# An attention block with a gated MLP: folding the softmax sums on GpSimd, and a new order of the first projections

## The chip, the cores and the metric

The kernel runs on one core of a Trainium2 chip. The metric is the device time of one launch in microseconds (us), the median of several runs. Engines in the profile: PE is TensorE (PEld its weight loads), DVE is VectorE, ACT is ScalarE, POOL is GpSimd, SPq is the queue that issues transfers.

## The reference, cut to what matters

```python
h = layernorm(x) * (1 + ca) + sa                  # x: 2048 rows of 1024, bf16; modulation from c @ w_mod
q = (h @ wq) as 32 heads of 32;  k = h @ wk;  v = h @ wv     # one key and value head for all
p = softmax(q k^T / sqrt(32));   o = p v
x = x + ga * (o @ wo)
h = layernorm(x) * (1 + cb) + sb
x = x + gb * ((silu(h @ w1) * (h @ w3)) @ w2)      # 3584 wide
```

Two pieces set the work: 2048 x 2048 exponentials for each of 32 heads (ScalarE), and the matmuls (TensorE).

## The kernel before

The queries are taken in eight blocks of 256 rows, the heads in eight groups `f` of four. One step is one score tile pair: 8 score matmuls of two key tiles against four heads, and two exps of 128x1024 that write a tile of 128x2048 in bf16. Eight steps make a head group. The MLP of one block runs as filler between the scores of the next.

A program at build time simulates the engines with assumed durations and fixes, for each engine, the order of its instructions. On the chip every engine works through its list in that order, with waits on semaphores. So an assumed duration decides only about order; the chip decides about time.

The softmax denominator is the sum of the exps over keys. VectorE first adds exp tiles in two trees of four, then folds the second tree into the first; TensorE multiplies the result with a matrix of ones and zeros (`SEL`) to sum over partitions:

```python
# in step(): the tree
G.add("dve", ... TR[tr] = U[first] + U[u] ...)            # L942
G.add("dve", ... TR[tr] = TR[tr] + U[u] ...)              # L948
# ...
def finish(f, h=None):
    trs = trees[f]
    if h is None and f in FOLD:                            # FOLD = groups 0 to 6
        ta, tb = trs
        G.add("dve", lambda e, ta=ta, tb=tb: e.tensor_tensor(
            TR[:, ta, 0:4 * W], TR[:, ta, 0:4 * W], TR[:, tb, 0:4 * W], ALU.add), ...)   # L957, 128x2048
        trs = trs[:1]
    # ... the value matmuls of this group, then the sums of the group before:
    def dmm(e, ...):
        for x in range(len(td) * npk):                     # npk = 2 key tiles side by side
            for gg in range(4):
                e.matmul(PB[g.bank][32 * gg:32 * gg + 32, qn:2 * qn], SEL[:, ga, gj, :],
                         a[:, (gg * npk + x % npk) * qn:...], ..., tile_position=(0, 32 * gg))
```

The kernel uses eight banks of PSUM, the on-chip memory that the matmuls here write to; SBUF is the other one, which holds inputs and results. While attention runs, six banks hold scores and two (`PB0`, `PB1`) serve everything else: the filler matmuls, the values and the sums. VectorE empties these two.

The softmax here doesn't subtract the row's maximum and nothing guards it: scores larger than these inputs give would overflow.

## Time and profile before

| | kernel before |
|---|---|
| time, median of 3 runs before the prediction | 1160.13 us (1158.57 to 1160.46) |
| span of the profiled run | 1158.1 us |
| first exp, last exp | 29.2 us, 1047.7 us |
| a full block of 256 queries | 126.1 us |
| TensorE, ScalarE, VectorE busy in it | 125.7, 125.6, 117.0 us |
| after the last exp | 110.4 us, TensorE alone |

The table's rows are read from the busy time by stage and from the timeline of the exps; the prediction shows the lines. The VectorE groups are rows of the instruction table: line, engine, operation, output and inputs, shapes, count, then total busy us, mean ns of one, and idle time before them.

```profile
L948 DVE TENSOR_TENSOR UREG<-UREG 128x2048 bf16<-128x2048 bf16 x240 | 292.8, 1220 | 12.8 <-ACT UREG L925 10.8
L942 DVE TENSOR_TENSOR UREG<-UREG 128x2048 bf16<-128x2048 bf16 x120 | 146.4, 1220 | 11.5 <-PE PB L1002 6.4 <-ACT UREG L925 5.0
L1158 DVE SCALAR_TENSOR_TENSOR HREG<-GSB,HREG 128x512 bf16<-128x512 bf16 x56 | 38.4, 685 | 0.3
L1153 DVE TENSOR_TENSOR HREG<-GSB,PB 128x512 bf16<-128x512 bf16 x52 | 35.5, 683 | 3.3 <-PE PB L1141 3.2
L1042 DVE TENSOR_TENSOR QT<-XN 128x256 bf16<-128x256 f32 x64 | 26.7, 421 | 0.3
L1124 DVE TENSOR_SCALAR QT<-QT,MODC 128x256 bf16<-128x256 bf16 x48 | 13.2, 342 | 0.0
```

Read the input side: `UREG`, `XN`, `QT`, `GSB`, `HREG` lie in SBUF, `PB` in PSUM. The tree adds, the gating product L1158 and the division L1042 have two inputs in SBUF; L1153 has one in SBUF and one in PSUM; the scaling L1124 has one tensor input, in SBUF.

### The profile page before, as it was taken

To read this page: it belongs to the slowest core of one execution; us is meant where nothing else is said; L and a number is where in the kernel's file an instruction comes from. 1 tells how busy PE (TensorE), PEld (TensorE's weight loads), DVE (VectorE), ACT (ScalarE), POOL (GpSimd) and SP (SyncE) were. 2 spreads that over 40 slices of the span, in tenths; PEclk is the share of its full clock that TensorE was granted. 3 is DMA by queue.
4 is the path that set the end of the run, shared out by engine and by line. 5 is a ranking of instruction groups with operands and counts; after the bars stand their busy time and mean duration, and the time that the engine had idled before them with its cause. 6 is when DMAs were issued, how large, how long until landed. Compare 5 with 4: busy or idle time off the path is not lost.

```text
span 1158.1 us, 35702 instructions
## 1 busy us (share of the span) xinstructions
PE 1122.6 (97%) x15918; PEld 767.1 (66%) x15918; DVE 984.7 (85%) x1498; ACT 1027.6 (89%) x1170; POOL 43.5 (4%) x86
## 2 busy tenths in 40 slices
PE   7799998999979999999999999999999999999998
PEld 6564444776646766777577766776677766777887
DVE  5837889999888999899999998999989999997452
ACT  5789999999999999999999999999999999992110
POOL 3200001000000001000100001000100010000000
PEclk8899999999989999999999999999999999999999
DMA  9337005956546565856496567766586649756996
GB/s 331 113 129 220 19 2 127 275 169 178 166 122 190 169 193 149 248 170 192 119 279 196 159 177 194 226 169 174 152 252 181 185 122 258 204 152 192 284 291 160
DMA packets 385417, 211.10 MB, mean 182 GB/s; under 512 B 21744, under 2 KB 376048, under 8 KB 385264
## 3 DMA queue, kind: packets, MB, share of 16 engines
q1 hardware_dynamic: 383184, 208.69, 64.5%
q8 instruction: 125, 2.05, 0.8%
q10 hardware_dynamic: 2080, 0.13, 0.1%
q14 instruction: 28, 0.23, 0.1%
HBM read 201.46 MB, written 4.19 MB: 178 GB/s over the span
## 4 chain that ended last, share of the span: by engine, by line
PE 92%; ACT 3%; DVE 3%; DMA 1%; SPq 1%; issue 0%; POOL 0%; DVEq 0%
PE PB L1141 33%; PE PB L1175 16%; PE SP L915 14%; PE PB L975 11%; PE PB L1107 5%; PE PB L658 4%; PE SP L1141 3%; ACT UREG L925 3%; PE SP L1175 2%; PE PB L1002 2%; DMA UREG<-in_w_mod_dram 1%; PE PB L637 1%; PE PB L838 0%; PE SP L1107 0%; DVE WO L850 0%
## 5 line engine op out<-in xcount | busy, mean ns | idle before, releaser
L925 ACT ACTIVATE UREG<-SP 128x1024 bf16<-128x1024 f32 x1024 | 968.6, 1075 | 18.8 <-PE SP L915 16.4
L948 DVE TENSOR_TENSOR UREG<-UREG 128x2048 bf16<-128x2048 bf16 x240 | 292.8, 1220 | 12.8 <-ACT UREG L925 10.8
L915 PE MATMUL SP<-QT,KT 32*128 32x256 bf16 x4096 | 204.8, 274 | 16.0 <-ACT UREG L925 15.0
L1141 PE MATMUL PB<-QT,WREG 128*128 128x256 bf16 x1648 | 207.4, 274 | 1.8 <-DVE DSB L1026 1.6
L1141 PEld LDWEIGHTS PB<-QT,WREG 128*128 128x128 bf16 x1648 | 150.1, 98 | 46.8 <-issue 31.2
L942 DVE TENSOR_TENSOR UREG<-UREG 128x2048 bf16<-128x2048 bf16 x120 | 146.4, 1220 | 11.5 <-PE PB L1002 6.4
L915 PEld LDWEIGHTS SP<-QT,KT 32*128 32x128 bf16 x4096 | 61.2, 93 | 138.6 <-ACT UREG L925 79.6
L1141 PE MATMUL PB<-QT,HREG 128*128 128x256 bf16 x1056 | 133.7, 274 | 0.8 <-DVE DSB L1026 0.8
L975 PE MATMUL PB<-UREG,V 128*32 128x256 bf16 x4032 | 132.2, 277 | 1.7 <-DVE QT L610 0.9
L975 PEld LDWEIGHTS PB<-UREG,V 128*32 128x32 bf16 x4032 | 99.3, 98 | 27.5 <-issue 17.9
L1141 PEld LDWEIGHTS PB<-QT,HREG 128*128 128x128 bf16 x1056 | 96.1, 98 | 29.7 <-issue 19.6
L1175 PE MATMUL PB<-WREG,HREG 128*128 128x256 bf16 x812 | 101.2, 273 | 0.0
L1175 PEld LDWEIGHTS PB<-WREG,HREG 128*128 128x128 bf16 x812 | 75.3, 98 | 20.4 <-issue 11.4
L1175 PE MATMUL PB<-HREG 128*128 128x256 bf16 x532 | 67.8, 274 | 0.0
L1141 PE MATMUL PB<-QT,X 128*128 128x256 bf16 x528 | 67.8, 274 | 0.0
L658 PE MATMUL PB<-HREG,WREG 128*128 128x512 bf16 (+1 forms) x312 | 64.1, 343 | 0.3 <-DVE DSB L1026 0.3
L957 DVE TENSOR_TENSOR UREG<-UREG 128x2048 bf16<-128x2048 bf16 x52 | 63.4, 1220 | 0.5
L1150 ACT ACTIVATE GSB<-GSB 128x512 bf16<-128x512 bf16 x56 | 38.8, 693 | 27.5 <-DVE GSB L1148 27.5
L1014 DVE COPY XN<-PB 128x256 f32<-128x256 f32 x63 | 26.6, 422 | 39.6 <-PE PB L1002 39.3
L1175 PEld LDWEIGHTS PB<-HREG 128*128 128x128 bf16 x532 | 49.2, 98 | 14.3 <-issue 8.0
L1107 PE MATMUL PB<-WO,QT 128*128 128x512 bf16 x232 | 57.6, 381 | 0.2 <-DVE QT L661 0.2
L1141 PEld LDWEIGHTS PB<-QT,X 128*128 128x128 bf16 x528 | 48.2, 98 | 14.3 <-issue 9.3
(139 smaller groups left out, 1031.9 us busy)
## 6 DMA issues: line engine op xcount, KB each, us to landing
WREG<-in_B_w_dram SPq DMA_DIRECT2D x112, 512.0 KB, 5.1
HREG<-in_B_w_dram SPq DMA_DIRECT2D x74, 512.0 KB, 5.2
WREG<-in_B_w_dram SPq DMA_DIRECT2D x33, 896.0 KB, 5.1
X<-in_B_w_dram SPq DMA_DIRECT2D x38, 512.0 KB, 5.1
HREG<-in_B_w_dram SPq DMA_DIRECT2D x21, 896.0 KB, 5.2
X<-in_B_w_dram SPq DMA_DIRECT2D x10, 896.0 KB, 5.1
X<-in_A_x_dram SPq DMA_DIRECT2D x32, 256.0 KB, 5.0
WREG<-in_w_mod_dram SPq DMA_DIRECT2D x16, 512.0 KB, 4.7
```

Of the source, the lines that this page charges most:

```text
L658: g = mm_group(NC, lambda e, b, c: e.matmul(b[:, 0:n], WQ[:, c, f * P:(f + 1) * P], HT[:, c, sl], start=c == 0, stop=c == NC - 1), lambda ...
L915: r = e.matmul(SP[:, b, o:o + qn], KT[32 * gg:32 * gg + 32, kts[j] * P:(kts[j] + 1) * P], QT[32 * gg:32 * gg + 32, f, q0:q0 + qn], start=T ...
L925: G.add("act", lambda e, u=u, h0=h0, n=n, b0=b0, nb=nb: e.activation(U[:, u, h0 * W:(h0 + n) * W].rearrange("p (b w) -> p b w", b=nb), SP[ ...
L942: G.add("dve", lambda e, tr=tr, u=u, fu=first_u: e.tensor_tensor(TR[:, tr, 0:4 * W], U[:, fu, 0:4 * W], U[:, u, 0:4 * W], ALU.add), reads= ...
L948: G.add("dve", lambda e, tr=tr, u=u: e.tensor_tensor(TR[:, tr, 0:4 * W], TR[:, tr, 0:4 * W], U[:, u, 0:4 * W], ALU.add), reads=[("TR", tr) ...
L957: G.add("dve", lambda e, ta=ta, tb=tb: e.tensor_tensor(TR[:, ta, 0:4 * W], TR[:, ta, 0:4 * W], TR[:, tb, 0:4 * W], ALU.add), reads=[("TR", ...
L975: r = e.matmul(PB[g.bank][32 * gg:32 * gg + 32, 0:qn], V[:, kt, :], U[:, pu, (gg * npk + j) * qn:(gg * npk + j + 1) * qn], start=w0 + n == ...
L1014: G.add("dve", lambda e, g=g, f=f: e.tensor_copy(ASB[:, f % 4, 0:qn], PB[g.bank][:, 0:qn]), writes=[("ASB", f % 4), ("XN", 2 + f % 4 // 2) ...
L1107: g = mm_group(NC, lambda e, b, f, t=t, h=h: e.matmul(b, QT[:, f, t * P:(t + 1) * P], WO[:, f, h * 512:(h + 1) * 512], start=f == 0, stop= ...
L1141: return e.matmul(b[:, j * qn:(j + 1) * qn], w13[:, w, c, j * P:(j + 1) * P], QT[:, c, q0:q0 + qn], start=c == 0, stop=c == NC - 1)
L1150: G.add("act", lambda e, b=b: e.activation(TB[b], GS[b], ACT.Tanh, scale=0.5), reads=[("GS", b)], writes=[("TB", b)], clear=alias("TB") if ...
L1175: G.add("pe", lambda e, g=g, j=j, fc=fc, hf=hf, first=first, w2s=w2s: e.matmul(PB[g.bank][:, j * 256:(j + 1) * 256], HHT[:, hf * NH + fc, ...
```

## The change

It has two parts. First, 48 of 52 folds move from VectorE to GpSimd, which is idle, as two adds of half the width; a third GpSimd add folds the two key tiles side by side, so that TensorE streams 4 sum matmuls per head group instead of 8. Second, the first projections: priorities of the first queries, bias adds and late layer norms, the PSUM banks of the first key projections, and warm-up matmuls of 512 columns instead of 128.

```diff
+    POOLT = 0.0022                               # assumed us per element on GpSimd
+    DFOLD = [(QB, f) for f in range(4)]          # four folds stay on VectorE
...
             if h is None and f in FOLD:
                 ta, tb = trs
-                G.add("dve", lambda e, ta=ta, tb=tb: e.tensor_tensor(
-                    TR[:, ta, 0:4 * W], TR[:, ta, 0:4 * W], TR[:, tb, 0:4 * W], ALU.add), ...)
+                pool = (q0, f) not in DFOLD
+                parts = 2 if pool else 1
+                for k in range(parts):
+                    a, b = k * 4 * W // parts, (k + 1) * 4 * W // parts
+                    G.add("pool" if pool else "dve", lambda e, ta=ta, tb=tb, a=a, b=b: e.tensor_tensor(
+                        TR[:, ta, a:b], TR[:, ta, a:b], TR[:, tb, a:b], ALU.add), ...)
+                if pool and npk == 2:
+                    tv = TR[:, ta, 0:4 * W].rearrange("p (g j q) -> p g j q", g=4, j=2)
+                    G.add("pool", lambda e, tv=tv: e.tensor_tensor(tv[:, :, 0], tv[:, :, 0], tv[:, :, 1], ALU.add), ...)
+                    nx = 1
...
-                    for x in range(len(td) * npk):
+                    for x in range(len(td) * nx):
...
-    kproj(512, 512, (1,))
+    kproj(512, 512, (6, 7))
...
-    qproj(0, 256, 1, (0, 1))
+    qproj(0, 256, 1, (0, 1), prio=1)
     vproj(0, (0, 1))
+    qproj(0, 256, 2, (0, 1), prio=1)
     vproj(1, (0, 1))
...
-    G.warm = (WARM, P / 2400.0 + 0.0026, warm, ident)
+    G.warm = (WARM, MM, warm, ident, 26.0)
```

(Cuts marked with "..."; left out are priorities and the plumbing of `nx`.)

## The prediction

> **What bounds the kernel now.** I read the page's busy table first, then the busy time by stage. The eight query blocks of 256 rows have a period of 126.1 us, so I cut the windows at the first exp (29.2), at the block starts and at the last exp (1047.7). Columns: stretch, length, PE, PEld, DVE, ACT, POOL busy, granted clock, DMA share, GB/s.
>
> ```profile
> PE 1122.6 (97%) x15918; PEld 767.1 (66%) x15918; DVE 984.7 (85%) x1498; ACT 1027.6 (89%) x1170; POOL 43.5 (4%) x86
> ```
>
> ```profile
> 29.20:62.00 32.80, 26.37 (x556) 17.24 (x556) 26.36 (x72) 22.61 (x25) 6.65 (x16) 0.90 0.42 119
> 62.00:184.00 122.00, 117.34 (x1763) 59.80 (x1756) 89.67 (x138) 119.36 (x127) 0.00 (x0) 1.00 0.26 82
> ...
> 310.50:436.60 126.10, 117.14 (x1669) 77.52 (x1665) 114.20 (x166) 124.39 (x142) 3.48 (x4) 0.96 0.59 164
> ...
> 562.70:688.80 126.10, 125.70 (x1812) 85.84 (x1804) 117.04 (x171) 125.59 (x143) 3.43 (x4) 1.00 0.69 189
> ...
> 1047.70:1158.10 110.40, 106.00 (x1012) 91.57 (x1009) 53.03 (x95) 10.94 (x19) 1.69 (x4) 1.00 0.89 233
> ```
>
> The reader sees two engines full at once: in a steady block TensorE is busy 125.7 and ScalarE 125.6 of 126.1 us. VectorE has 9 us free, GpSimd nearly all. After the last exp TensorE alone runs 110 us (rest of the seventh MLP, the last block). So the end is: last exp, plus the TensorE work left then. Over all stages TensorE idles 35.5 us, and ScalarE 18.3 us between first and last exp. The timeline says where:
>
> ```profile
> 35.60 7.44 ACT L925 ACTIVATE UREG<-SP 128x1024 bf16<-128x1024 f32 x8 [2.56 <-PE SP L915]
> ...
> 61.86 19.00 ACT L925 ACTIVATE UREG<-SP 128x1024 bf16<-128x1024 f32 x20 [5.57 <-PE SP L915]
> ...
> 325.16 0.40 PE L915 MATMUL SP<-QT,KT 32*128 32x256 bf16 x8 [1.43 <-ACT UREG L925]
> 326.99 0.40 PE L915 MATMUL SP<-QT,KT 32*128 32x256 bf16 x8 [1.44 <-ACT UREG L925]
> ```
>
> In the head ScalarE starves (10.2 us between 29 and 62, half of it one gap before 61.86), because projections and transposes stand ahead of the scores in TensorE's order. At 325 the reverse: seven score steps stand without filler between them, and TensorE waits 1.2 to 1.4 us at each.
>
> **What the Trainium skill says.** "SBUF — State Buffer", section "Who interferes with whom": VectorE and GpSimd share one port pair; a VectorE instruction with two SBUF inputs, or in a 2-port mode, and a GpSimd instruction that reads SBUF exclude each other for the whole instruction. The trace agrees in one direction:
>
> ```profile
> 569.85 1.23 DVE L942 TENSOR_TENSOR UREG<-UREG 128x2048 bf16<-128x2048 bf16 x1
> 569.99 1.16 POOL L551 TENSOR_SCALAR RS<-MV 128x1 f32<-128x1 f32 x1 [119.41 <-DVE MV L532]
> ...
> 1064.42 0.22 POOL L551 TENSOR_SCALAR RS<-MV 128x1 f32<-128x1 f32 x1 [109.39 <-DVE MV L532]
> ```
>
> The same one-column instruction takes 0.22 us alone and 1.16 beside an add, ending when the add ends. The other direction, a long GpSimd instruction that stops an add, does not occur here: no GpSimd work is long enough.
>
> "GPSIMD Engine Reference", section 3.1 "Elementwise — side-by-side cycle accounting": about 2.6 cycles per element for a two-input add at 1.2 GHz, so by estimate 1024 x 2.6 / 1.2 = 2.2 us for 1024 elements. No such add is in the trace.
>
> "TensorE: Matmul & The Clock Gate", Part 1: an idle window of some 3.4 us halves the clock. The trace agrees roughly: scores of 0.40 us become 0.61 after the waits at 325, and the clock of that stage is 0.96, in the head 0.90.
>
> **The change, part by part.**
>
> 1. *Sum matmuls.* The built order has 608 against ones instead of 800: for 48 of 52 folded head groups, 4 instead of 8. Four run side by side in array columns, and of the same shape
>
> ```profile
> L1002 PE MATMUL PB<-UREG,SEL 128*32 128x256 bf16 x776 | 31.8, 275 | 0.0
> ```
>
> ```profile
> 148.94 1.86 PE PB L975 x64
> ```
>
> the chain of waits gives 1.86 / 64 = 29 ns each (the 275 of the first line, a group of the instruction table, is latency). Removed: 192 x 29 ns = **5.6 us** of TensorE, 0.8 us per block. All of it lies in the full stage.
>
> 2. *Folds.* VectorE loses 48 adds of 1.22 us (58.6 us; 8 per block). GpSimd gains 96 half-adds and 48 key-tile adds, each of 1024 elements: 144 x 2.2 = 317 us by the estimate, 46 per block. GpSimd's own share, 4% to about 31%, is no bound. A fold of 3 x 2.2 = 6.6 us instead of 1.2 has to be done by the next head group's sums, one period of 126.1 / 8 = 15.8 us later, so latency alone is hidden.
>
> 3. *Order of the first projections.* Queries 1 to 3 rise to scores' rank, their bias adds go first on VectorE, late layer norms too. In the built order the first MLP tanh comes after 184 exps instead of 168, so scores run 8 steps further ahead; the run of seven bare score steps at 325 is one of three. I expect the 5.6 us gap to close and about 2.5 of the other 4.6 us in the head: **-8 us** at ScalarE. The first score has the same work in front of it, so 29.2 stays. Warm-up matmuls of 512 columns, a little closer packed, only fill idle time; I give them nothing of their own.
>
> 4. *Tail.* After the last score matmul stand 45 gate/up matmuls where there were 2 (and 20 sum matmuls for 24). The chain has 80 of them in 8.73 us, 0.109 us each: 43 x 0.109 = **+4.7 us** of filler moved behind the last exp.
>
> *Sums.* ScalarE's side: -8 in the head, -2 from smaller waits in five full blocks (at most 126.1 - 125.6 = 0.5 each), +4.7 in the tail: -5.3 us. TensorE's side: -5.6 sums, -5.8 for four bare steps fewer at 1.44, some -2 of idle in the head: -13. Both must be met; the later one sets the end. ScalarE's -5.3 would be 1155; but how much of its 10 us in the head closes is my least certain term (all 10.2 would give -7.5, 1152.6). I choose 7 us gain: **1153 us**.
>
> **Rivals.**
>
> *A, the shared port makes VectorE the bound.* In the steady block, VectorE work that needs the pair is: tree adds 58.6, gating products 9.6, divisions 3.4, residual adds 1.7, two-port scalings 3.3: 77 us. With 46 us of GpSimd that is 123 of 126 us under one lock. VectorE's room is 9 idle + 8 removed = 17 us, or 0.8 us for each of the 21 GpSimd pieces of a block. If each piece holds VectorE for what remains after one short PSUM instruction (0.7 us; 2.2 - 0.7 = 1.5 us), 31 us are lost and 14 not covered: over six or seven blocks +80 to +100, about 1240. For it: the exclusion seen above, two thirds of the block's VectorE time needing the pair. Against it: about half the VectorE instructions (80 of 171 in the block) have at most one SBUF input and can run beside GpSimd; seen so far is only GpSimd waiting; the folds are cut in halves and four are left on VectorE in one block, as if somebody had measured; a tuned kernel rarely takes a step that costs 7%. A milder form: each hold delays a PSUM read, and TensorE, with two PSUM banks for filler and 0.4 us of slack per block, cannot catch up; 0.1 us per piece is 2 us per block, 14 in all: 1165.
>
> *B, nothing gained: ScalarE is the bound anyway.* In full blocks it has 0.5 us free, so the 5.6 us of matmuls could turn into idle TensorE time and the head's gain be handed back in the tail: 1158 to 1161. For it: 125.6 of 126.1 busy. Against it: TensorE alone fills the last 110 us and its total work counts there.
>
> *C, the head closes wholly.* ScalarE's idle time of 18.3 us shrinks to 3 or 4 and the clock does not drop: last exp 14 us earlier, +4.7: 1149 to 1151, a few us less if cold time is won back.
>
> **Range and chances.** Main line and C span 1147 to 1157, B to 1161, the milder A to 1168. Eight in ten: 1143 to 1168. Full A gets 9%; below 1137 needs more than 20 us, more than ScalarE's idle time allows even with the tail unchanged: 3%. Within 2%: 88%.
>
> **What would show it.** Right: sum matmuls' busy time down by a quarter; exps without a gap over 3 us from 29 on; last exp at 1037 to 1042; block period 125.6 to 126.1; GpSimd's adds near 2.2 us, VectorE's adds still near 1.22; some 115 us after the last exp. A: adds of VectorE over 2 us, VectorE near 100% busy or idle at GpSimd's release, a longer block period, TensorE waiting for VectorE or GpSimd before projections and sums. B: TensorE idle in steady blocks up by 0.8 us, the end unmoved. C: the stage 29 to 62 with ScalarE over 90% busy. The prediction is wrong above all if GpSimd's instructions hold VectorE for their whole length, or if they take much longer than 2.2 us because they wait for VectorE, so that the sums come late.

## The result, and the profile after

The changed kernel takes **1266.82 us** (1264.17 to 1268.32, 4 runs) against 1159.35 us in the same rounds: 9.2% slower, ratio 1.0924, 95% interval 1.0907 to 1.0941. (A ratio here is the mean time of one kernel's runs over that of the other's in the same rounds, so not quite the ratio of the medians quoted.)

The page's busy line, then four stages, cut at the first and the 129th exp, and later near every further 128th (within two exps), in the columns of the prediction's table of stages:

```profile
PE 1144.6 (91%) x15643; PEld 756.4 (60%) x15643; DVE 1084.3 (86%) x1450; ACT 1033.8 (82%) x1170; POOL 394.9 (31%) x230
```

```profile
27.50:156.80 129.30, 117.72 (x1987) 64.30 (x1987) 94.83 (x168) 119.86 (x130) 27.92 (x25) 0.99 0.35 112
156.80:292.70 135.90, 125.36 (x1690) 75.06 (x1689) 127.98 (x170) 127.46 (x144) 25.84 (x13) 0.99 0.53 143
...
581.10:724.80 143.70, 129.47 (x1793) 85.19 (x1785) 133.78 (x161) 126.59 (x144) 55.10 (x25) 0.98 0.61 168
...
1147.40:1262.40 115.00, 110.55 (x1049) 95.31 (x1046) 56.96 (x101) 11.39 (x20) 1.58 (x4) 1.00 0.88 234
```

The first line: VectorE has 48 adds fewer and is busy 100 us longer. The stages: the first block's exps end at 156.8, before 162.4, so the head won time, and the last stage is 4.6 us longer, as reckoned. The whole loss sits between, in blocks of 135 to 147 us instead of 126 to 127. The second block, where four folds stayed on VectorE, is the shortest of these (134.9 from its first exp to the next block's; the line above has one exp more). But the seventh, with all its folds on GpSimd, takes only 135.9, so the blocks do not show what leaving four folds is worth. In a block of 143.7 us VectorE is busy 133.8 us for less work than the 117.0 of before.

The instruction table of the changed kernel names the instructions that grew. L955, L949, L1176, L1171, L1060 and L1142 are L948, L942, L1158, L1153, L1042 and L1124 of before:

```profile
L955 DVE TENSOR_TENSOR UREG<-UREG 128x2048 bf16<-128x2048 bf16 x240 | 345.9, 1441 | 4.9 <-ACT UREG L932 2.3
L949 DVE TENSOR_TENSOR UREG<-UREG 128x2048 bf16<-128x2048 bf16 x120 | 181.5, 1513 | 6.1 <-ACT UREG L932 4.8 <-PE PB L1020 0.9
L1176 DVE SCALAR_TENSOR_TENSOR HREG<-GSB,HREG 128x512 bf16<-128x512 bf16 x56 | 46.4, 828 | 0.8
L1171 DVE TENSOR_TENSOR HREG<-GSB,PB 128x512 bf16<-128x512 bf16 x53 | 35.7, 674 | 6.3 <-PE PB L1159 6.2
L1060 DVE TENSOR_TENSOR QT<-XN 128x256 bf16<-128x256 f32 x64 | 43.1, 679 | 0.4
L1142 DVE TENSOR_SCALAR QT<-QT,MODC 128x256 bf16<-128x256 bf16 x48 | 25.0, 582 | 1.2 <-DMA QT<-XN 1.2
```

Every group here with two SBUF inputs grew: the mean of an add from 1220 to 1441 and 1513 ns, of the division from 421 to 679. So did the scaling, 342 to 582. L1171, with one input in PSUM, did not: 683 and 674. A mean hides what happens to one; the timeline shows it (start, duration, engine):

```profile
598.01 2.13 POOL L969 TENSOR_TENSOR UREG<-UREG 128x1024 bf16<-128x1024 bf16 x1
598.24 2.98 DVE L949 TENSOR_TENSOR UREG<-UREG 128x2048 bf16<-128x2048 bf16 x1
600.22 2.98 POOL L975 TENSOR_TENSOR UREG<-UREG 128x1024 bf16<-128x1024 bf16 x1
601.32 2.95 DVE L955 TENSOR_TENSOR UREG<-UREG 128x2048 bf16<-128x2048 bf16 x1
...
631.38 7.81 DVE L1142 TENSOR_SCALAR QT<-QT,MODC 128x256 bf16<-128x256 bf16 x8
631.54 4.35 POOL L969 TENSOR_TENSOR UREG<-UREG 128x1024 bf16<-128x1024 bf16 x2 [4.90 <-DVE UREG L955]
635.97 2.12 POOL L975 TENSOR_TENSOR UREG<-UREG 128x1024 bf16<-128x1024 bf16 x1
...
639.45 0.40 DVE L1044 TENSOR_TENSOR DSB<-DSB,PB 128x256 f32<-128x256 f32 x1
639.99 1.22 PE L1159 MATMUL PB<-QT,WREG 128*128 128x256 bf16 x5 [6.39 <-DVE DSB L1044]
```

The VectorE add begins at 598.24, while GpSimd's runs from 598.01 to 600.14, and ends at 601.22: its own time (1.1 us of the usual 1.2) starts when GpSimd's instruction is through. Then GpSimd's next, begun at 600.22, lasts 2.98 instead of 2.13, for it waits in its turn. The two take turns. Below, eight scalings that need some 2.7 us take 7.81 while three GpSimd adds run; the copy out of a PSUM bank behind them is late, and TensorE, which needs the bank, stands for 6.39 us. So the time reaches the end: TensorE's waits for VectorE add up to 91.6 us (before: 12.1), ScalarE's waits for scores to 75.6 (before: 16.4). Part of the loss may come by the clock: the score matmuls right after that wait take 0.61 us instead of 0.40, the mean granted clock of the run is 0.978 (before: 0.990; short adds, below: 0.996), and TensorE is busy 1144.6 us where the same list takes 1116.0 with short adds. How much of the loss that makes is not shown.

Against a simpler story: TensorE waits for GpSimd's sums almost never. Of the folds the trace says (who waited, us, times):

```profile
  PEld PB L1020: 0.4, 2
```

### The profile page after: what moved, and what is told of

It is laid out like the page before. It is cut to its first block, busy times and chain, and to the rows that moved or that the text cites. A ratio compares the mean times of both kernels' runs of the same rounds, so it can differ in the third digit from the quotient of the medians.

```text
span 1262.4 us, 35193 instructions
## 1 busy us (share of the span) xinstructions
PE 1144.6 (91%) x15643; PEld 756.4 (60%) x15643; DVE 1084.3 (86%) x1450; ACT 1033.8 (82%) x1170; POOL 394.9 (31%) x230
## 4 chain that ended last, share of the span: by engine, by line
PE 44%; DVE 32%; ACT 12%; issue 9%; POOL 1%; DMA 1%; SPq 1%; DVEq 0%
PE PB L1159 13%; ACT UREG L932 11%; DVE UREG L955 10%; PE PB L1193 6%; PE SP L922 6%; DVE UREG L949 5%; PE PB L993 5%; PE SP L1193 3%; PE SP L1159 3%; PE PB L1125 3%; PE PB L660 3%; DVE HREG L1171 2%; DVE HREG L1176 2%; DVE QT L1142 2%; DVE QT L1060 2%
## 5 line engine op out<-in xcount | busy, mean ns | idle before, releaser
L932 ACT ACTIVATE UREG<-SP 128x1024 bf16<-128x1024 f32 x1024 | 965.1, 1054 | 77.2 <-PE SP L922 75.6
L969 POOL TENSOR_TENSOR UREG<-UREG 128x1024 bf16<-128x1024 bf16 x96 | 221.7, 2309 | 641.8 <-DVE UREG L955 638.4
L955 DVE TENSOR_TENSOR UREG<-UREG 128x2048 bf16<-128x2048 bf16 x240 | 345.9, 1441 | 4.9 <-ACT UREG L932 2.3
L1159 PE MATMUL PB<-QT,WREG 128*128 128x256 bf16 x1632 | 212.0, 277 | 36.3 <-DVE HREG L1171 10.0
L949 DVE TENSOR_TENSOR UREG<-UREG 128x2048 bf16<-128x2048 bf16 x120 | 181.5, 1513 | 6.1 <-ACT UREG L932 4.8
L1159 PE MATMUL PB<-QT,HREG 128*128 128x256 bf16 x1072 | 141.2, 278 | 17.0 <-DVE HREG L1171 9.2
L975 POOL TENSOR_TENSOR UREG<-UREG 128x1024 bf16<-128x1024 bf16 x48 | 130.3, 2714 | 3.4
L1193 PE MATMUL PB<-WREG,HREG 128*128 128x256 bf16 x728 | 92.4, 273 | 0.8 <-DVE HREG L1171 0.6
L1193 PEld LDWEIGHTS PB<-WREG,HREG 128*128 128x128 bf16 x728 | 66.9, 98 | 21.8 <-issue 12.1
L1125 PE MATMUL PB<-WO,QT 128*128 128x512 bf16 x232 | 60.9, 390 | 14.4 <-DVE X L1129 6.4
L660 PE MATMUL PB<-HREG,WREG 128*128 128x512 bf16 (+1 forms) x312 | 67.5, 350 | 4.0 <-DVE QT L663 2.1
L1168 ACT ACTIVATE WREG<-WREG 128x512 bf16<-128x512 bf16 x56 | 36.6, 654 | 42.1 <-DVE WREG L1166 42.0
```

Of the source, the lines that this page charges most:

```text
L660: g = mm_group(NC, lambda e, b, c: e.matmul(b[:, 0:n], WQ[:, c, f * P:(f + 1) * P], HT[:, c, sl], start=c == 0, stop=c == NC - 1), lambda ...
L932: G.add("act", lambda e, u=u, h0=h0, n=n, b0=b0, nb=nb: e.activation(U[:, u, h0 * W:(h0 + n) * W].rearrange("p (b w) -> p b w", b=nb), SP[ ...
L949: G.add("dve", lambda e, tr=tr, u=u, fu=first_u: e.tensor_tensor(TR[:, tr, 0:4 * W], U[:, fu, 0:4 * W], U[:, u, 0:4 * W], ALU.add), reads= ...
L955: G.add("dve", lambda e, tr=tr, u=u: e.tensor_tensor(TR[:, tr, 0:4 * W], TR[:, tr, 0:4 * W], U[:, u, 0:4 * W], ALU.add), reads=[("TR", tr) ...
L969: G.add("pool" if pool else "dve", lambda e, ta=ta, tb=tb, a=a, b=b: e.tensor_tensor(TR[:, ta, a:b], TR[:, ta, a:b], TR[:, tb, a:b], ALU.add),
L975: G.add("pool", lambda e, tv=tv: e.tensor_tensor(tv[:, :, 0], tv[:, :, 0], tv[:, :, 1], ALU.add), reads=[("TR", ta)], writes=[("TR", ta)], ...
```

## The experiments

Eleven kernels were run, each timed against the kernel before. My theory after the result: **the port**. A GpSimd instruction that reads SBUF and a VectorE instruction with two SBUF inputs exclude each other, each hold delays VectorE, and the delay is passed on. Rivals: **order** (the new order of the projections costs the time), **late sums** (the folds take too long), **bad list** (the fixed lists are poor, whatever GpSimd does), and later **room** (VectorE's idle time should have covered the holds).

### Order alone, folds alone

```diff
-                pool = (q0, f) not in DFOLD
+                pool = False                     # e1; e2 is the kernel before with the fold's hunks only
```

> All folds back on VectorE, the new order of the first projections and the longer warm-up matmuls kept: the order alone. Port theory (GpSimd's reads exclude VectorE's two-input instructions): no long GpSimd work, so VectorE's adds are 1.22 us again and the time is 1150 to 1158, a little below the kernel before, because the first 128 exps of the changed kernel were done 5.6 us earlier (156.8 against 162.4). Rival 'order': the new order costs the 107 us, so this run takes about 1266. Rival 'late sums': 1150 to 1158 as well.

> The kernel before with only the folds moved to GpSimd (and the single sum per head group). Port theory: 1260 to 1275, blocks of 140 to 147 us, VectorE's adds at a mean of 1.44 to 1.5 us. Rival 'order': about 1155. Rival 'late sums': 1260 to 1275 too, but with TensorE's waits for GpSimd before the sums adding up to tens of us.

Order alone: **1155.49 us**, correct, ratio 0.9966 (0.9949 to 0.9982). Folds alone: **1269.85 us**, correct, ratio 1.0945. The whole loss belongs to the folds; the order is a small gain. The rival "order" is out. The version with the order alone beats both kernels.

### GpSimd busy, but reading nothing; reading, but briefly

```diff
-    e.tensor_tensor(TR[:, ta, a:b], TR[:, ta, a:b], TR[:, tb, a:b], ALU.add)
+    e.memset(TR[:, ta, a:b], 1.0); e.memset(TR[:, tb, a:b], 1.0)                    # e3 (third add alike)
+    e.tensor_tensor(TR[:, ta, a:a+8], TR[:, ta, a:a+8], TR[:, tb, a:a+8], ALU.add)   # e4 (third add alike)
```

> The changed kernel, same order, but each GpSimd piece writes two runs of 1024 elements with a constant instead of adding (wrong result on purpose), so GpSimd is busy for about as long and the sums wait for it as before, but it reads nothing. Port theory: VectorE's adds back at 1.22 us, time 1148 to 1160. Rival 'late sums' (the length of GpSimd's work delays the sums): about 1266, unchanged. Rival 'bad list' (the fixed order of the engines' instructions, built with the folds off VectorE, is slow by itself): about 1266.

> The changed kernel, same order, but each GpSimd add covers 8 columns instead of 1024 (wrong result on purpose): GpSimd reads, but only for a moment. Port theory: 1148 to 1156, with adds at 1.22 us; this is what the change would have given without the exclusion. Late sums: the same. Bad list: about 1266.

Results wrong on purpose. Writing only: **1158.97 us**; short adds: **1157.30 us**. The lists of TensorE, VectorE and ScalarE are the changed kernel's. The instruction table of the first:

```profile
L955 DVE TENSOR_TENSOR UREG<-UREG 128x2048 bf16<-128x2048 bf16 x240 | 292.1, 1217 | 10.5 <-ACT UREG L932 8.7
L969 POOL MEMSET UREG<- 128x1024 bf16 x192 | 177.7, 954 | 627.5 <-DVE UREG L955 624.9
L976 POOL MEMSET UREG<- 128x1024 bf16 x96 | 89.0, 956 | 2.5
L1143 DVE TENSOR_SCALAR QT<-QT,MODC 128x256 bf16<-128x256 bf16 x48 | 18.4, 565 | 1.1 <-DMA QT<-XN 1.1
```

GpSimd works 177.7 + 89.0 = 267 us, in pieces of 1.9 us, somewhat less than the 352 of the changed kernel, and the sums wait for it as before; yet adds are at 1217 ns. Each piece is two writes of 0.95 us; that shortness alone does not save them is shown by g3 below, where 192 reading adds of 1.15 us, with 48 longer ones, still cost 87 us. So neither the length of the folds nor the list does the harm: "late sums" and "bad list" are out, and it is the reading that excludes. Two lines differ: the scalings are still slow at 565 ns (their longest is 1.17 us, in the run with short adds 0.35), and so is the normalization L575, of one tensor input in SBUF as well, at 712 ns against 539. They conflict with writes too.

The short adds measure what the change would give if GpSimd's reads cost nothing: 1157.3, a little above the 1148 to 1156 that I expected, and 2.5 us below the kernel before. It is not faster than the order alone (1155.5): in this list, the single sum per head group, 192 matmuls fewer, gains nothing that reaches the end. The busy line of the short adds, from which the next table starts:

```profile
PE 1116.0 (97%) x15613; PEld 756.0 (65%) x15643; DVE 936.8 (81%) x1450; ACT 1026.2 (89%) x1170; POOL 73.6 (6%) x230
```

### How much, for how many and how long

```diff
+                pool = f in (1, 3, 5)            # f1: 66 pieces instead of 144
+                pool = False; "if npk == 2:"     # f2: fold on VectorE, key tiles on GpSimd, 52 pieces
+                parts = 1                        # f3: fold as one GpSimd add of 2048 elements
+                parts = 4 if pool else 1         # g3: as four of 512
```

> The changed kernel with only head groups 1, 3 and 5 folded on GpSimd: 66 GpSimd pieces instead of 144, 9 in a full block instead of 21. The changed kernel is 109.5 us above the run with short adds (1266.8 - 1157.3), 0.76 us for each of 144 pieces. Theory 'each hold is passed on': 1157 + 66 x 0.76 = 1207. Rival 'VectorE has room' (my prediction's reckoning: up to its idle time, some 12 us per block here, holds cost nothing): 9 holds of about 1 us fit, 1155 to 1162.

> Folds of 2048 elements on VectorE, only the fold of the two key tiles (1024 elements) on GpSimd: 52 pieces, 7 in a full block. Each hold passed on: 1157 + 52 x 0.76 = 1197. VectorE has room: about 1156.

> The changed kernel with the GpSimd fold as one instruction of 2048 elements instead of two of 1024 (96 pieces, 48 of them twice as long). If the exclusion lasts for the whole instruction, single VectorE adds of up to 1.2 + 4.2 = 5.4 us are to be seen, and the time is 1265 to 1290. If the lock is given up inside an instruction, the longest add stays near 3.1 us, as now, and the time does not move.

> The changed kernel with each fold as four GpSimd adds of 512 elements (192 of 1.1 us and the 48 key-tile folds as they were). One piece cost 1291, two 1267. If the damage goes with the length of one hold, since a short VectorE instruction or a gap covers part of each, four pieces give 1245 to 1258. If it goes with the total time of GpSimd's reads, 1262 to 1272. The longest division would be near 0.2 + 2.1 us still, because of the key-tile folds.

All are correct. VectorE's extra time is its busy time less that of the run with short adds (936.8 us; for the first two rows less the VectorE folds that they have in addition: f1 26 x 1.22 us, as it has 30 where the short adds have 4; f2 by comparison with the order alone, 990.0 us). "Later" is the time less 1157.3 us (for f2 less 1155.5). The busy lines of the order alone, then of f2, f1, g3 and f3:

```profile
PE 1116.2 (97%) x15810; PEld 762.6 (66%) x15839; DVE 990.0 (86%) x1498; ACT 1026.1 (89%) x1170; POOL 38.1 (3%) x86
PE 1120.0 (96%) x15594; PEld 752.5 (64%) x15627; DVE 1023.7 (87%) x1498; ACT 1027.4 (88%) x1170; POOL 160.2 (14%) x138
PE 1129.6 (94%) x15722; PEld 757.7 (63%) x15751; DVE 1030.0 (86%) x1476; ACT 1027.5 (86%) x1170; POOL 208.2 (17%) x152
PE 1143.3 (92%) x15613; PEld 757.3 (61%) x15643; DVE 1059.6 (85%) x1450; ACT 1034.5 (83%) x1170; POOL 441.3 (35%) x326
PE 1149.0 (89%) x15610; PEld 768.1 (59%) x15643; DVE 1113.4 (86%) x1450; ACT 1034.9 (80%) x1170; POOL 372.5 (29%) x182
```

| run | GpSimd pieces | time | VectorE's extra | later | passed on |
|---|---|---|---|---|---|
| f2, key tiles only | 52 of 1024 | 1171.76 | 34 | 16 | 0.48 |
| f1, three of seven groups | 66 of 1024 | 1199.44 | 61 | 42 | 0.69 |
| g3, four pieces | 192 of 512, 48 of 1024 | 1244.20 | 123 | 87 | 0.71 |
| changed kernel | 144 of 1024 | 1266.82 | 148 | 110 | 0.74 |
| f3, one piece | 48 of 2048, 48 of 1024 | 1291.12 | 177 | 134 | 0.76 |

Three things follow. The loss does not wait for VectorE to be full: with 9 pieces in a block, which by the rival "room" should have cost nothing, f1 is 42 us late; some 0.7 to 0.76 of the hold time arrives at the end. Only where one piece comes alone, in f2, is it half, and there my 1197 was too high. And the damage goes with the length of one hold: the same elements cost 134 us in one piece, 110 in two, 87 in four (the times with one and with four lie about 1 us outside the ranges that I expected, above and below). The lists of these runs were computed anew, while those of the short adds are the changed kernel's; so a part of each "later" may be the list's, and how much is not shown (f4 and g1 below show what a list can do). In the run with one piece the divisions show how long a hold is (shortest, median and longest in ns):

```profile
L1060 DVE TENSOR_TENSOR QT<-XN x64: 361/420/4276, 92.1 to 1188.5; 128x256 bf16<-128x256 f32 x64
```

The longest, 4.28 us, is the usual 0.42 and nearly the whole of a GpSimd add of 4.07 us (median there). In the changed kernel the longest is 2.34, with GpSimd adds of 2.13. The exclusion lasts for a whole instruction. The adds themselves, for which I had expected up to 5.4 us, reached 3.96.

### The key-tile fold on VectorE

```diff
-                if pool and npk == 2:
-                    G.add("pool", lambda e, tv=tv: e.tensor_tensor(...), ...)
+                if npk == 2:                     # and pool = False
+                    G.add("dve", lambda e, tv=tv: e.tensor_tensor(...), ...)
```

> No GpSimd folds: both folds on VectorE, so 52 adds of 1024 elements, some 0.6 us each (4 us per block), are added there and the sum matmuls fall to 592. If TensorE's time counts, 1150 (5.6 us below the order alone, 1155.5). If ScalarE bounds the blocks, as the short-adds run suggests, 1155 to 1158: the single sum is worth nothing.

**1162.19 us**, correct, ratio 1.0022: slower than either expectation, and 6.7 us slower than the order alone. The stage after the last exp of the order alone, then of this run:

```profile
1038.70:1152.80 114.10, 109.67 (x1043) 94.59 (x1042) 55.29 (x98) 11.41 (x20) 1.58 (x4) 0.99 0.89 233
```

```profile
1036.80:1160.20 123.40, 118.88 (x1124) 102.84 (x1123) 60.75 (x105) 13.20 (x23) 1.58 (x4) 1.00 0.90 234
```

The last exp is 1.9 us earlier, and 9.3 us more work stands behind it: the list computed with a fuller VectorE has put filler off to the tail, where TensorE works alone. Between the exps TensorE idled instead (in the fifth block it is busy 120.8 of 126.4 us). So fewer sum matmuls made room that this list did not fill; what another list would make of them is not shown.

### Honest durations, and the warm-up

```diff
-  dur=dve_t(4 * npk * qn, 2), prio=TREEP)
+  dur=dve_t(4 * npk * qn, 2) + 0.25, prio=TREEP)   # g1, the other held instructions alike
-  G.warm = (WARM, MM, warm, ident, 26.0)
+  G.warm = (WARM, P / 2400.0 + 0.0026, warm, ident) # g2: the order alone with the old warm-up
```

> The changed kernel with honest durations in the fixed order: the order of the engines' lists is computed with VectorE's adds 0.25 us longer, its gating products 0.18, divisions 0.25 and scalings 0.24, and the key-tile fold on GpSimd 0.5 us longer, near the means measured in the changed kernel. If the loss comes from lists made for VectorE times that do not hold, it falls by 20 us or more, to below 1247. If it is the holds themselves, wherever they fall, 1255 to 1280.

> The order alone (1155.5) with the old warm-up matmuls of 128 columns: splits the head's gain. The first exp was 1.7 us earlier with the new warm-up (27.5 against 29.2), with the same matmuls ahead of it, so 1157 if the warm-up gave that and the new priorities the rest; 1160 if the warm-up gave all of the 4.3 us.

With the durations told: **1361.80 us**, correct, and outside both expectations. The holds stayed (adds at a mean of 1473 and 1659 ns), but the new list, reckoning with a full VectorE, left 229 us of work behind the last exp at 1131. The list is thus a second lever of its own, and this run does not say how well a list could be fitted to the holds; that stays open. It does show that the holds are there under another list too.

With the old warm-up: **1158.04 us**. Of the 4.3 us that the order gains, the warm-up matmuls give 2.5 (give or take 1.6, from the spread of four runs each) and the priorities the rest. The first exp agrees: it starts at 29.4 us here and at 27.6 with the new warm-up.

## Why the prediction was wrong

- **The step that failed is the cost of the folds to VectorE, and behind it rival A's room.** The main line, 1153, lets the folds cost VectorE nothing: part 2 takes 58.6 us off it and adds no hold. I had the exclusion, its evidence in one direction and the class of instructions right, but only as a rival with 9%. There the wrong term is "VectorE's room is 9 idle + 8 removed = 17 us", to be set against holds of 31 us a block. The holds were smaller than that: VectorE's extra 147.5 us over 144 pieces is 1.02 us for each, 21 in a block, against the 1.5 that I put in. But only a quarter was covered: 0.76 us a piece, 16 us a block, reached the end. So it was luck that "about 1240" came near: a hold too long and a room too large nearly cancel (14 us a block not covered, against 16). In this kernel idle time is not a store to draw on: a hold can fall in front of a copy that frees one of two PSUM banks, as at 639 us, while the idle time lies elsewhere.
- **The argument that outweighed the reckoning was about authors, not about the chip**: folds cut in halves, "as if somebody had measured". The halves do help (1267 against 1291), and that says nothing about whether the move to GpSimd does.
- **"The trace agrees in one direction" was the place to stop.** The page "SBUF — State Buffer" of the Trainium skill, section "Who interferes with whom", says that whoever starts first holds the port pair for the whole instruction. The trace of before showed GpSimd waiting for an add; the trace of after shows the other half, an add of 2.98 us and a division of 2.34 beside a GpSimd add of 2.13. I had written of GpSimd's reads alone; the scalings slowed by writes (565 ns) show that for these the exclusion is wider.
- **The milder form was the right mechanism in the wrong size**: I let it cost 0.1 us per piece; it was 0.76.
- **GpSimd's durations held.** I estimated 2.2 us for 1024 elements; undisturbed adds take 2.12 to 2.13. GpSimd's share is 31%, as said, and the sums do not come late (0.4 us of waiting).
- **The order's part had the right sign, at about a third of its size.** Without the exclusion the change gives 1157.3, a gain of 2.5 us where I chose 7. Last exp 6.8 us earlier (1040.9 in the run with short adds) where I took 10; tail longer by 4.9 us, where I had 4.7. My sum for ScalarE, -5.3, was nearer than the -7 that I chose. "29.2 stays" failed: the first exp starts at 27.5, and the warm-up matmuls, to which I gave nothing, did it.
- **The -5.6 us for the sum matmuls never arrives.** That fits rival B, though its sign, more idle time of TensorE, is not shown clearly: with short adds a full block still takes 126.1 us, with ScalarE busy 125.4 and TensorE 125.2 of them, and the run without the single sum (1155.5) is at least as fast as those with it (1157.3, 1162.2), in lists that differ.
- **The clock was read too easily.** No idle window of 3.4 us stands in the stretch at 325: the waits are 1.2 to 1.44 us, with 0.40 us of scores between them, and the scores slow to 0.61 us all the same. The agreement is weaker than I wrote, and many short waits of TensorE went with a slower clock here.

## What to carry to other kernels

Before work moves to GpSimd, count which VectorE instructions have two SBUF inputs or a one-input form in SBUF that is slowed by GpSimd's writes as well, and expect each GpSimd read to hold them for its whole length. Do not pay for the holds out of VectorE's idle share: here about 0.7 to 0.76 of the hold time reached the end in four of five runs, although VectorE, without the holds, is idle for some 18 of 126 us in a block (busy 108.1 with short adds). When a rival is backed by a mechanism that the trace shows by half, reckon its time and give it its weight, and test it by running the same list with GpSimd writing instead of reading.

## What the Trainium skill lacked or had wrong

- "SBUF — State Buffer", section "Who interferes with whom": right in both directions and in its classes (adds of 1.22 us up to 3.17 in the kernel with GpSimd reads, at 1.22 beside writes; scalings of 0.34 up to 1.17 us beside writes). It lacks a measured case of VectorE held by a GpSimd add: 0.42 us became 2.34 and 4.28, as GpSimd's instruction was 2.13 or 4.07 us long.
- The same section does not say that cutting the GpSimd instruction into pieces lessens the damage: 1291, 1267 and 1244 us for one, two and four pieces.
- "GPSIMD Engine Reference", section 3.1: its figure is for fp32. In bf16 an add takes 1.15 us for 512, 2.13 for 1024 and 4.07 for 2048 elements, so by estimate 2.4 to 2.7 cycles an element at its 1.2 GHz: its 2.6 serves for bf16 too.
- No page says how little of such holds VectorE's idle time covers when the engines' lists are fixed: 69 to 76% of the hold time was passed on in four runs, 48% in one.
